# A state-space and gated-GELU layer: half-precision rows turned by DMA instead of by TensorE

## The chip, the cores and the metric

The kernel runs on one core of a Trainium2 chip. The metric is the device time of one execution in microseconds (us), given as the median of several runs. Engines are TensorE (PE), VectorE (DVE), ScalarE (ACT), GpSimd (POOL) and SyncE (SP); SP here only issues DMA transfers.

## The reference, cut to what matters

A sequence x of 2048 rows with 448 channels passes two stages, each behind an adaptive layer norm (scale and shift from a condition vector):

```
h = layernorm(x) * (1 + ca) + sa
x = x + ga * S4(h)                        # long convolution over the sequence, by FFT
h = layernorm(x) * (1 + cb) + sb
g = h @ w_gate ; u = h @ w_up             # 448 -> 1792
x = x + gb * ((gelu(g) * u) @ w_down)     # 1792 -> 448
```

The change lies in the second stage, between the second layer norm and the products with `w_gate` and `w_up`.

## The kernel before

**Stages.** Up to about 385 us the kernel makes the convolution's spectra and the convolution itself. Then the second stage goes through the 2048 rows in four blocks of 512 (`blk` 0 to 3; the change's "blocks two to four" are `blk` 1 to 3). Each block has four row groups of 128 rows (`j` 0 to 3).

**What happens to one row group** (`conv_out`, L1378 to L1494): the last step of the inverse transform on PE and the residual add (L1405 to L1419); the norm on VectorE into a float32 tile `xn` (L1450, task `co.nx`); then the split into two half-precision numbers in one tile `hl` of 128 x 1024. `split_hi` (L1455, task `co.h2`) writes the rounded value into columns 0 to 511, on ScalarE or VectorE as the order says; `split_lo` (L1460, task `co.l2`) writes what is left over into columns 512 to 1023, always on VectorE (a subtraction of 448 columns and a copy of 64). The products need the rows with channels on partitions. So `tr16` (L1466, task `co.t2`) turns the eight 128 x 128 pieces of `hl` on PE into a PSUM tile `pt`, and `out_` (L1473, task `co.c2`) copies that tile into slot `j` of `ht`, a tile of 128 x 8 x 4 x 128 (copies at L481 are ScalarE's, at L483 VectorE's).

**What uses it.** `gate_up` (L1496) makes 14 products per block (`f` 0 to 13; blk 0 does its first four in two halves). A product has 20 matmuls of 128 x 128 by 512 columns (L1528) and four smaller ones (L1522) into the PSUM pair `pq`. ScalarE takes the GELU (L1535), VectorE multiplies (L1542) into `fq`, and `fq` is split once more into `hh` (ScalarE, L1554) and `hlo` (VectorE, L1557) for the product with `w_down` (`down_first` for blk 0, L1597; `down` for the others, L1628 and L1688).

**Buffers.** `hl` has two buffers, `xn` three, `pt` two, `ht` one: a new tile waits until the last reader of the one before it in the ring is done. All but `pt` lie in one pool (`w0`), which is laid over memory that earlier stages have given back.

**Order.** Nothing is scheduled at run time. Every task has a place in the table `PLACE`, and `Plan.order` (L296) sorts all tasks by it; each engine runs its own tasks in that order and waits at each for what it needs. A letter behind a place chooses the engine (a, d, p, s). So blk 1's preparation is woven into blk 0's products: on PE, the last products of blk 0 have places 1549, 1560, 1570 and 1578, the transposes of blk 1 have 1568 (j = 0), 1577 (j = 2), 1590 (j = 3) and 1593 (j = 1), and the first product of blk 1 has 1596. In blk 2 and 3 the row groups are prepared while PE does `down` of the block before.

**SP's queue.** SP issues most transfers, in the order of places too, and stands still at one that must wait. Around blk 1's transposes these are the loads of down weights (`d.ld`, L1735: 1538, 1555, 1569, 1585), a load of gate weights (L1333: 1542), a reload of split weights (`wr.ld`, L1368: 1563, into the three-deep ring `wr`), their store (L1360: 1586) and the next block's convolution result (L1279: 1598).

Of the kernel before, what the change touches and what calls it, by code (L numbers as in the profile page):

```python
# [12 lines left out]
HF = mybir.dt.float16  # L13
# [399 lines left out]
def s4_geglu(ctx: ExitStack, tc: tile.TileContext, a: dict, out: bass.AP):  # L413
    nc = tc.nc
    dma = nc.sync.dma_start
# [31 lines left out]
    POOLS = {"gz": gzs.enter_context(tc.tile_pool(name="gz", bufs=1, side="right")),  # L447
             "ua": uas.enter_context(tc.tile_pool(name="ua", bufs=2, side="right", reuse_waits="tile"))}
# [24 lines left out]
    def add(n, eng, v, fn, deps=(), alloc=(), use=(), table=None, kb=0.0, soft=()):  # L473
        t = plan.add(n, eng, v, fn, list(deps) + list(soft) + [EV.get(GATE.get(b.tag)) for b in alloc], alloc, use, table, kb)
        t.soft = set(soft)
        return t
    EXP, TRIG, ATAN, SQRT, LN = ("exp",), ("trig",), ("atan", "trig"), ("sqrt",), ("ln",)

    def cp(e, dst, src):
        if e == "ACT":  # L480
            A.activation(dst, src, AF.Copy)  # L481
        else:
            V.tensor_copy(dst, src)  # L483

    def sp(n, v, dst, src, kb, deps=(), alloc=(), use=(), q="SP"):
        qf = adma if q == "ACT" else dma
        return add(n, {q: 0.42 if q == "SP" else 0.1}, v, lambda: qf(dst(), src()), deps, alloc, use, kb=kb)
# [890 lines left out]
    def conv_out(blk, t_x, t_y):  # L1378
        xb, yb, hb = X1[blk], YI[blk], Buf("ht")
# [53 lines left out]
        for js in sets:  # L1433
# [9 lines left out]
            t3 = add("co.rc" + z, {"DVE": 0.15}, v0 + js[-1] + 0.3, inv, [t2])  # L1443
            for j in js:
                rst[j] = t3
        cps = []
        for j in range(4):
            xn, pt, hl = Buf("xn"), Buf("pt" if blk else "pd"), Buf("hl")

            def norm(j=j, xn=xn):  # L1450
                xn.tile = POOLS["w0"].tile([128, D], FT, name="xn", bufs=3)
                V.scalar_tensor_tensor(xn.tile, xb.tile[:, j], MV[blk][1][:, j, 0:1], cb1, op0=OP.subtract, op1=OP.mult)
                V.scalar_tensor_tensor(xn.tile, xn.tile, RS[blk][:, j:j + 1], sb, op0=OP.mult, op1=OP.add)

            def split_hi(e, xn=xn, hl=hl):  # L1455
                hl.tile = POOLS["w0"].tile([128, 1024], HF, name="hl")
                cp(e, hl.tile[:, :D], xn.tile)
                cp(e, hl.tile[:, D:512], xn.tile[:, 384:])

            def split_lo(xn=xn, hl=hl):  # L1460
                V.tensor_sub(hl.tile[:, 512:512 + D], xn.tile, hl.tile[:, :D])
                V.tensor_copy(hl.tile[:, 512 + D:], hl.tile[:, 896:512 + D])

            pts = [pt, pt if blk else Buf("pd")]

            def tr16(k0=None, pts=pts, hl=hl):  # L1466
                b = pts[1 if k0 else 0]
                n, k0 = (8, 0) if k0 is None else (4, k0)
                b.tile = POOLS["pd" if n == 4 else "pt"].tile([128, n, 128], HF, name="pd" if n == 4 else "pt")
                for k in range(n):  # L1470
                    T.transpose(b.tile[:, k], hl.tile[:, 128 * (k0 + k):128 * (k0 + k) + 128], K2["ih"])

            def out_(e, k0=None, j=j, pts=pts):  # L1473
                if j == 0 and not k0:
                    hb.tile = POOLS["w0"].tile([128, 8, 4, 128], HF, name="ht", bufs=1)
                ks = slice(0, 8) if k0 is None else slice(k0, k0 + 4)
                cp(e, hb.tile[:, ks, j], pts[1 if k0 else 0].tile)
            vj = v0 + (j + 0.5 if blk == 0 else j + 4.5)
            t1 = add("co.n" + z, {"DVE": 1.38}, vj, norm, [rst[j]], [xn], [xb])
            if blk:  # L1480
                t2 = add("co.h2", {"ACT": 0.8, "DVE": 0.5}, vj + 0.1, split_hi, [t1], [hl], [xn])
                t3 = add("co.l2", {"DVE": 0.7}, vj + 0.2, split_lo, [t2], (), [xn, hl])
                t4 = add("co.t2", {"PE": 0.55}, vj + 0.3, tr16, [t3, c_ih], [pt], [hl])
                cps.append(add("co.c2", {"ACT": 1.05, "DVE": 0.75}, vj + 0.4, out_, [t4] + cps[:1], [hb] if j == 0 else [],
                               [pt] + ([hb] if j else [])))
                continue
            t2 = add("co.h0", {"ACT": 0.7, "DVE": 0.47}, vj + 0.1, split_hi, [t1], [hl], [xn])
            t3 = add("co.l0", {"DVE": 0.8}, vj + 0.2, split_lo, [t2], (), [xn, hl])
            t4 = add("co.ta", {"PE": 0.3}, vj + 0.2, lambda tr16=tr16: tr16(0), [t2, c_ih], [pt], [hl])
            t5 = add("co.ca", {"ACT": 0.5, "DVE": 0.42}, vj + 0.3, lambda e, out_=out_: out_(e, 0), [t4] + cps[:1], [hb] if j == 0 else [],  # L1490
                     [pt] + ([hb] if j else []))
            t6 = add("co.tb", {"PE": 0.3}, vj + 0.3, lambda tr16=tr16: tr16(4), [t3, t4], [pts[1]], [hl])
            cps += [t5, add("co.cb", {"ACT": 0.5, "DVE": 0.42}, vj + 0.4, lambda e, out_=out_: out_(e, 4), [t6, t5], (), [pts[1], hb])]
        CO[blk] = cps  # L1494

# [114 lines left out]
    def down(blk):  # L1610
# [91 lines left out]
        def put(m):  # L1702
# [10 lines left out]
    c_ih = sp("c.ih", 58, lambda: K2["ih"], lambda: a["k_ih"], 32, [EV["end"]])  # L1713
    t_x = x1_load(0, [EV["end"]])
    t_w = add("warm", {"ACT": 0.25}, 58, lambda: A.activation(dump, eps, AF.Sqrt), [EV["end"]], table=SQRT)
    conv_out(0, t_x, YL)
    spin(6, [EV["pq"], c_ih], Buf("pq"), None, lambda: POOLS["ps"].tile([128, 512], FT, name="pq0"),
         lambda t: (K2["ih"], K2["ih"][:, None].to_broadcast([128, 4, 128]), t.rearrange("p (a b) -> p a b", b=128)))
# [39 lines left out]
    for blk in range(4):  # L1758
        for half in range(2 if blk == 0 else 0):
            for f in range(HALF):  # L1760
                gate_up(blk, f, half)
        if blk == 0:
            down_weights(False)
        f0 = 0 if blk else HALF
        for f in range(f0, 14):
            if f % 2 == 0:
                w_load(blk, f // 2) if blk else f // 2 < PRE or weights(f // 2)
            gate_up(blk, f)
            if f == 0 and blk == 1:
                down_weights(True)  # L1770
            if f == f0 and blk < 3:
                conv_out(blk + 1, x1_load(blk + 1, [CO[blk][-1]]), [yi_load(blk + 1)])
        if blk:
            down(blk)
            continue
        for j in range(4):
            down_first(j)
# [54 lines left out]
```

## Time and profile before

| | |
|---|---|
| runs | 796.06, 799.72 and 801.69 us, median 799.72 |
| profiled execution | span 793.8 us from the first to the last instruction; its page gives no further time of its own |
| busy | PE 731.5 us (92%), DVE 594.2 (75%), ACT 466.6 (59%), POOL 9.0 (1%) |
| granted clock of TensorE | 0.995 of full speed over the span |
| DMA | 136.74 MB, mean 172 GB/s |
| the 96 transposes into `pt` (L1471) | 7.0 us of PE busy, between 453.5 and 692.8 us |
| the 12 copies out of `pt` | 7 on ACT of 1.02 us, 5 on DVE of 0.69 us (medians) |

How to read it: a row of a timeline has start, duration, engine, line, operation, what is written from what is read, the shape and how many; in brackets stands how long the engine was idle before it and what ended that. "PEld" is the loading of weights into TensorE, which overlaps with matmuls. The chain of work that ended last has rows of start, duration and what ran; "issue" there is time in which the engine waited for nothing that the profile shows. "SPq" is SP's DMA queue: its rows are the issuing, not the transfer. PE's matmuls overlap, so the chain, which counts each only once, is the view to read PE's time from.

### The profile page before, as it was taken

To read this page: it belongs to the slowest core of one execution; us is meant where nothing else is said; L and a number is where in the kernel's file an instruction comes from. 1 tells how busy PE (TensorE), PEld (TensorE's weight loads), DVE (VectorE), ACT (ScalarE), POOL (GpSimd) and SP (SyncE) were. 2 spreads that over 40 slices of the span, in tenths; PEclk is the share of its full clock that TensorE was granted. 3 is DMA by queue.
4 is the path that set the end of the run, shared out by engine and by line. 5 is a ranking of instruction groups with operands and counts; after the bars stand their busy time and mean duration, and the time that the engine had idled before them with its cause. 6 is when DMAs were issued, how large, how long until landed. Compare 5 with 4: busy or idle time off the path is not lost.

```text
span 793.8 us, 19204 instructions
## 1 busy us (share of the span) xinstructions
PE 731.5 (92%) x8262; PEld 449.3 (57%) x8262; DVE 594.2 (75%) x896; ACT 466.6 (59%) x620; POOL 9.0 (1%) x24
## 2 busy tenths in 40 slices
PE   1866889998999999989999999999999999999998
PEld 0333444443677767678774445444695446944478
DVE  4989999999999999978868851569773587133743
ACT  5699998899999999952645530233412334212330
POOL 0000000000000000002100000000000000000000
PEclk9999999999999999999999999999999999999999
DMA  9554559998888757988797563355307222012201
GB/s 270 172 150 143 152 148 243 284 277 235 232 252 228 219 176 240 299 308 214 234 275 246 205 173 112 127 174 172 131 13 220 93 93 93 2 47 92 82 1 59
DMA packets 91119, 136.74 MB, mean 172 GB/s; under 512 B 21716, under 2 KB 72596, under 8 KB 91034
## 3 DMA queue, kind: packets, MB, share of 16 engines
q1 hardware_dynamic: 85156, 127.32, 53.5%
q10 hardware_dynamic: 5318, 7.22, 2.9%
q8 instruction: 65, 1.06, 0.6%
q0 software_dynamic: 560, 0.98, 0.5%
q14 instruction: 20, 0.16, 0.1%
HBM read 100.39 MB, written 36.01 MB: 172 GB/s over the span
## 4 chain that ended last, share of the span: by engine, by line
PE 64%; DVE 6%; ACT 5%; DMA 3%; issue 3%; SPq 0%; DVEq 0%; ACTq 0%
PE pq L1528 28%; PE pq L1628 9%; PE pd L1597 4%; PE pf L1106 3%; PE kg L749 3%; PE pf L1095 2%; PE kg L772 2%; PE pg L676 2%; PE pq L1522 2%; DMA yi<-y 2%; DVE ty L726 2%; PE pd L1628 2%; PE pd L1405 1%; DVE tx L722 1%; DVE q L1099 1%
## 5 line engine op out<-in xcount | busy, mean ns | idle before, releaser
L1528 PE MATMUL pq<-ht,wr 128*128 128x512 f16 (+1 forms) x1200 | 248.6, 365 | 0.9 <-ACT ge L1535 0.9
L1528 PEld LDWEIGHTS <-wr 128*128 128x128 f16 x1200 | 114.5, 98 | 128.6 <-issue 12.0
L726 DVE TENSOR_TENSOR ty<-my,fg 128x2048 f32<-128x2048 f32 x56 | 127.5, 2283 | 0.9 <-ACT fg L700 0.3
L1542 DVE TENSOR_TENSOR fq<-ge,pq 128x512 f32<-128x512 f32 (+1 forms) x60 | 38.9, 649 | 72.7 <-PE pq L1528 45.6
L1535 ACT ACTIVATE ge<-pq 128x512 f32<-128x512 f32 (+1 forms) x60 | 34.0, 566 | 87.9 <-PE pq L1522 52.8
L1554 ACT ACTIVATE hh<-fq 128x1024 f16<-128x1024 f32 (+1 forms) x49 | 46.7, 961 | 62.2 <-DVE fq L1542 43.6
L1628 PE MATMUL pq<-d,hh 128*128 128x224 f16 x476 | 69.2, 259 | 0.0
L722 DVE TENSOR_TENSOR tx<-mx,fg 128x1024 f32<-128x1024 f32 x56 | 67.7, 1217 | 1.6 <-ACT fg L693 1.0
L749 PE MATMUL kg<-ty,tx 128*32 128x64 f32 x3584 | 62.7, 222 | 4.2 <-DVE tx L722 1.7
L749 PEld LDWEIGHTS kg<-ty,tx 128*32 128x32 f32 x3584 | 53.5, 111 | 22.4 <-issue 12.9
L1557 DVE TENSOR_TENSOR hlo<-fq,hh 128x1024 f16<-128x1024 f32 (+1 forms) x49 | 53.7, 1105 | 15.4 <-ACT hh L1554 15.2
L1628 PE MATMUL pq<-d,hlo 128*128 128x224 f16 x238 | 61.6, 259 | 0.0
L689 ACT ACTIVATE fg<-pg 128x1024 f32<-128x1024 f32 x56 | 58.2, 1039 | 0.8 <-PE pg L676 0.4
L663 ACT ACTIVATE my<-pg 128x1024 f32<-128x1024 f32 x56 | 55.7, 1032 | 2.1 <-PE pg L658 1.9
L1628 PEld LDWEIGHTS <-hh 128*128 128x128 f16 x560 | 54.0, 98 | 0.6 <-issue 0.2
L1106 PE MATMUL pf<-q,fc 128*128 128x160 f32 x264 | 41.5, 307 | 1.2 <-DVE q L1099 1.2
L693 ACT ACTIVATE fg<-fg,small 128x1024 f32<-128x1024 f32 x36 | 41.6, 1172 | 0.1
L1106 PEld LDWEIGHTS pf<-q,fc 128*128 128x128 f32 x264 | 36.4, 190 | 6.6 <-issue 1.5
L676 PEld LDWEIGHTS <-lt 64*128 64x128 bf16 x304 | 17.8, 94 | 37.6 <-issue 25.4
L1745 ACT ACTIVATE d<-fq 128x896 f16<-128x896 f32 x14 | 13.2, 945 | 43.1 <-PE pd L1597 27.3
L676 PE MATMUL pg<-ea,lt 64*128 64x512 bf16 x152 | 30.7, 387 | 7.2 <-ACT fg L700 3.2
L985 PE MATMUL pf<-ui,fu 128*128 128x448 f32 x66 | 31.1, 575 | 1.7 <-ACT uo L481 1.4
(212 smaller groups left out, 1141.3 us busy)
## 6 DMA issues: line engine op xcount, KB each, us to landing
wr<-w_d SPq DMA_DIRECT2D x21, 896.0 KB
fc<-in_k_fc SPq DMA_DIRECT2D x20, 576.0 KB
u_d<-so SPq DMA_DIRECT2D x32, 224.0 KB
ui<-u_d SPq DMA_DIRECT2D x10, 672.0 KB
fq<-in_wd SPq DMA_DIRECT2D x14, 448.0 KB
w<-in_wgu SPq DMA_DIRECT2D x11, 512.0 KB
us<-uo SPq DMA_DIRECT2D x22, 240.0 KB
q<-us SPq DMA_DIRECT2D x22, 240.0 KB
```

The lines of the kernel that those rows point to most:

```text
L663: A.activation(yb.tile.rearrange("p h (n k) -> p n h k", n=2), pb.tile.rearrange("p (n h k) -> p n h k", n=2, h=2), AF.Exp)
L676: T.matmul(pa[:, nh * 512:nh * 512 + 512], w, x, start=(k == 0), stop=(k == 2))
L689: A.activation(fb.tile[:, 0].rearrange("p x (n k) -> p n x k", n=2), pb.tile.rearrange("p (n x k) -> p n x k", n=2, x=2), AF.Sin, scale=TW ...
L693: A.activation(fb.tile[:, 1], fb.tile[:, 1], AF.Sin, scale=-TWO_PI, bias=halfpi)
L722: V.tensor_mul(tx.tile, xb.tile[:, xm, None, :].to_broadcast([128, 2, 512]), fb.tile[:, :, 0])
L726: V.tensor_mul(ty.tile, yb.tile[:, :, None, :].to_broadcast([128, 2, 2, 512]), fb.tile[:, None, :, 1].to_broadcast([128, 2, 2, 512]))
L749: T.matmul(kg[32 * g:32 * g + 32, 2 * (s % 2) + q, :64], tx[:, r, nh, 4 * q + g], ty[:, 0:4:3, nh, 4 * q + g] if r else ty[:, 1:3, nh, 4 * ...
L1106: T.matmul(pz.tile[:, e % 32 - sl0], fc.tile[:, i, 1 + t], pp.tile[:, t, i], start=(t == 0 and e != 32), stop=(t == 1 and e != 0))
L1528: T.matmul(pb.tile[k][:, ts], wr.tile[:, 4 * lo + t, k, c0:c0 + 128], ht[:, m, ts], start=f % 2 == 0 and i == 0, stop=f % 2 == 1 and i == 9)
L1554: A.activation(hg.tile[0][:, cb, c], fq.tile[:, c], AF.Copy)
L1557: V.tensor_sub(hg.tile[1][:, cb, c], fq.tile[:, c], hg.tile[0][:, cb, c])
L1628: T.matmul(bank(k)[:, m], x[:, p, q[0], ts], w[:, p, q[1]], start=new and m == 0 and p == 0 and z == 0, skip_group_check=True, stop=i in ( ...
```

## The change

For blk 1 to 3, the transposes on PE (`co.t2`) and the copies out of PSUM (`co.c2`) go away. In their place one DMA per row group, issued by SP, moves `hl` (128 x 1024, half precision, 256 KB) into slot `j` of `ht` and transposes its eight 128 x 128 pieces on the way. Each has the place of the `split_lo` before it (only blk 3's j = 2 has 1857 instead of 1851, behind j = 0). `hl` gets three buffers and `ht` two. Blk 0 keeps its transposes on PE.

```diff
-    "co.c2": "1588d 1594d 1589d 1592a 1760d 1762d 1774a 1773a 1892a 1906a 1901a 1900a",
...
-    "co.t2": "1568 1593 1577 1590 1756 1758 1769 1771 1877 1904 1868 1895",
+    "co.xt": "1541 1584 1573 1576 1753 1754 1763 1766 1857 1893 1857 1884",
...
             def split_hi(e, xn=xn, hl=hl):
-                hl.tile = POOLS["w0"].tile([128, 1024], HF, name="hl")
+                hl.tile = POOLS["w0"].tile([128, 1024], HF, name="hl", bufs=3)
...
+            def turned(j=j, hl=hl):
+                if j == 0:
+                    hb.tile = POOLS["w0"].tile([128, 8, 4, 128], HF, name="ht", bufs=2)
+                dma(hb.tile[:, :, j], hl.tile, transpose=True)
+
             def out_(e, k0=None, j=j, pts=pts):
                 if j == 0 and not k0:
-                    hb.tile = POOLS["w0"].tile([128, 8, 4, 128], HF, name="ht", bufs=1)
+                    hb.tile = POOLS["w0"].tile([128, 8, 4, 128], HF, name="ht", bufs=2)
...
                 t3 = add("co.l2", {"DVE": 0.7}, vj + 0.2, split_lo, [t2], (), [xn, hl])
-                t4 = add("co.t2", {"PE": 0.55}, vj + 0.3, tr16, [t3, c_ih], [pt], [hl])
-                cps.append(add("co.c2", {"ACT": 1.05, "DVE": 0.75}, vj + 0.4, out_, [t4] + cps[:1], [hb] if j == 0 else [],
-                               [pt] + ([hb] if j else [])))
+                cps.append(add("co.xt", {"SP": 2.0}, vj + 0.4, turned, [t3] + cps[:1], [hb] if j == 0 else [], [hl] + ([hb] if j else []), kb=256))
                 continue
```

## The prediction, made before the changed kernel was run

> **What bounds the kernel now.** I read the page first (spans and busy shares), then the chain of work that ended last from 385 us on, then the timelines of each engine around the transposes, the waits of the DMA queue and the DMA view of single stretches.
>
> ```profile
> span 793.8 us, 19204 instructions
> PE   1866889998999999989999999999999999999998
> ```
>
> TensorE (PE) is busy in nine tenths or more of nearly every slice. The edits touch only blocks two to four (code: blk 1 to 3), which come after 430 us, so their worth is read from the chain there (start, duration, what ran).
>
> ```profile
> 453.66 0.45 PE pt L1471 x8
> ...
> 458.74 0.57 PE pt L1471 x8
> ...
> 464.82 0.62 PE pt L1471 x8
> ...
> 465.47 1.02 ACT ht L481
> ...
> 467.00 4.48 PE pq L1528 x20
> ...
> 584.25 0.89 PE pt L1471 x16
> ...
> 593.19 0.89 PE pt L1471 x16
> 594.08 4.03 PE pq L1628 x42
> 598.11 4.32 PE pq L1528 x20
> ...
> 662.21 0.55 PE pt L1471 x8
> ...
> 692.55 0.45 PE pt L1471 x8
> ...
> 697.02 4.32 PE pq L1528 x20
> ```
>
> Two things are to be seen. The chain is PE nearly without a break, so whatever PE no longer does shortens the run one for one. And the L1471 groups are the transposes that go away: blk 1's four groups lie between 453 and 466 us, blk 2's (two at a time) at 584 and 593, blk 3's from 662 to 693 (four, of which the first and the last are shown; the two between are of 0.45 us like the last). The first gate-up product that needs the transposed rows starts at 467.00, 598.11 and 697.02.
>
> Only ahead of 467.00 does PE also stand still:
>
> ```profile
> 459.38 0.72 ACT L481 ACTIVATE hl<-xn 128x448 f16<-128x448 f32 x2 [4.03 <-PE pt L1471]
> 459.55 4.49 PE L1528 MATMUL pq<-ht,wr 128*128 128x512 f16 x20
> 461.08 1.22 DVE L1557 TENSOR_TENSOR hlo<-fq,hh 128x1024 f16<-128x1024 f32 x1 [2.83 <-ACT hh L1554]
> 462.23 0.62 DVE L1461 TENSOR_TENSOR hl<-xn,hl 128x448 f16<-128x448 f32 x1
> 462.88 0.18 DVE L1462 COPY hl<-hl 128x64 f16<-128x64 f16 x1
> 466.16 0.69 DVE L483 COPY ht<-pt 128x1024 f16<-128x1024 f16 x1 [0.20 <-PE pt L1471]
> ```
>
> The split of the last row group (j = 1) on ScalarE waits 4.03 us for a half-precision buffer ("hl", two of them) that PE's transposes release. Its second half on VectorE ends at 463.06. PE's last product of blk 0 ends at 464.04, then come transposes and copies, and only after the copy that ends at 466.85 does PE go on at 467.00. From 464.04 to 467.00 is 2.96 us, in which 16 transposes lie.
>
> **The change part by part.**
>
> *Removed from PE.* Blk 1: 0.45 + 0.57 + 2.96 = 3.98 us. Blk 2: 0.89 + 0.89 = 1.78. Blk 3: 0.55 + 3 x 0.45 = 1.90. Together 7.66 us, 0.96% of the span: the most that the change can give, since nothing else on the chain is touched.
>
> *Removed from VectorE and ScalarE.* Twelve copies of 0.69 or 1.02 us. They lie beside PE's work, apart from those of blk 1, which the 2.96 us already hold. I count the rest at nothing: PE covers them, and without that cover they would be worth the copies themselves, some 10 us, on engines that here wait for PE.
>
> *The third "hl" buffer, blk 1.* Rows to rebuild the time of the last split:
>
> ```profile
> 451.66 0.95 ACT L1745 ACTIVATE d<-fq 128x896 f16<-128x896 f32 x1 [1.95 <-DMA fq<-in_wd]
> 452.65 1.09 DVE L1748 SCALAR_TENSOR_TENSOR d<-fq,d 128x896 f16<-128x896 f32 x1 [1.02 <-ACT d L1745]
> 454.14 0.72 ACT L481 ACTIVATE hl<-xn 128x448 f16<-128x448 f32 x2 [1.53 <-PE pt L1471]
> ...
> 456.21 0.69 DVE L1453 SCALAR_TENSOR_TENSOR xn<-xn,rs,rows 128x448 f32<-128x448 f32 x1
> 456.82 0.68 DVE L1542 TENSOR_TENSOR fq<-ge,pq 128x512 f32<-128x512 f32 x1
> ...
> 460.01 1.04 ACT L1554 ACTIVATE hh<-fq 128x1024 f16<-128x1024 f32 x1
> ```
>
> The split of j = 2 need no longer wait till 454.14: ScalarE is free at 452.6 and done at 453.3. VectorE is free at 453.74 and makes j = 2's second half by 454.55 (0.80 us), j = 1's normalised row by 455.95 (1.4), the gate product by 456.6 (0.68), j = 3's second half by 457.4. ScalarE splits j = 1 at 456.0 and makes "hh" by 457.8 (1.04); VectorE makes "hlo" by 459.1 (1.22) and j = 1's second half by 459.9, where it was 463.06. So the last transfer of blk 1 can be issued at 459.9. PE, without 1.02 us of transposes, is ready for it at 464.04 - 1.02 = 463.0. The second "ht" buffer is what lets the transfers land while PE still reads blk 0's rows; with one, all four would have to wait till 463.0.
>
> *Memory.* The pool of these tiles grows by 8 KB ("ht") and 2 KB ("hl") per partition, so its tiles and those of the pools opened later lie over other tiles of the earlier stages, whose last readers they wait for. No row shows such a wait ahead of blk 1. I count it at nothing; one on the chain would cost its own length.
>
> *Added: twelve DMA transposes of 256 KB on SP's queue.* No transpose by DMA is in the trace, so its time x from issue to landing is bounded by plain transfers.
>
> ```profile
> 438.25 0.56 SPq L1735 DMA_DIRECT2D fq<-in_wd  x1
> 442.18 0.95 ACT L1745 ACTIVATE d<-fq 128x896 f16<-128x896 f32 x1 [0.80 <-DMA fq<-in_wd]
> 791.02 0.34 ACTq L1710 DMA_DIRECT2D out<-x  x1
> q1 hardware_dynamic: 85156, 127.32, 53.5%
> ```
>
> A load of 448 KB issued at 438.25 released a waiting ScalarE at 442.18: 3.9 us. The last store, 112 KB issued at 791.02, has landed before the span ends: under 2.8 us. On a straight line 256 KB take 3.3 us; 2.8 is the low end. The high end: the rows move in pieces of 128 halves, 256 bytes, so 1024 pieces, and the mean packet of queue 1 took 0.535 x 16 x 793.8 / 85156 = 0.080 us on one of 16 engines. That makes 5.1 us of transfer in place of about 1.3, and x = 7.1. I take x = 4.0, by the row that it is nearest to, the 448 KB load.
>
> [...]
>
> *Where they queue.*
>
> ```profile
> 439.55 0.34 SPq L1333 DMA_DIRECT2D w<-in_wgu  x1
> 440.21 0.18 DVE L1462 COPY hl<-hl 128x64 f16<-128x64 f16 x1
> 447.45 1.04 ACT L1346 ACTIVATE wr<-w 128x1024 f16<-128x1024 f32 x1
> 453.76 9.12 SPq L1735 DMA_DIRECT2D fq<-in_wd  x2
> ```
>
> SP issues in a fixed order and stands still at each transposing transfer until VectorE's second half is there. Blk 1's j = 0 waits till 440.4, and the weight load behind it, issued at 439.55 now, goes about 1.4 us later; ScalarE converts it only at 447.45. j = 2 goes at 454.6, right behind the load at 453.76; j = 3 at 457.4, j = 1 at 459.9. The load behind that one, the second of the row with 9.12 us, waits for the buffer that "hlo" frees (462.3 now, 459.1 then), and loses nothing.
>
> In blk 2 only stores of finished rows and the next convolution's load stand behind the transfers. In blk 3 the loads of the weight ring do:
>
> ```profile
> 654.63 0.63 DVE L1461 TENSOR_TENSOR hl<-xn,hl 128x448 f16<-128x448 f32 x1
> 657.60 0.32 SPq L1368 DMA_DIRECT2D wr<-w_d  x1
> ```
>
> Its j = 0 is ready at 655.5, 2.1 us ahead of the load at 657.60, which itself waits for PE: room for two issues of up to 1 us. I count this at nothing; an issue of 2 us would put that load off by 2 us, and PE still has two loaded weight blocks in the ring of three to work on.
>
> Blk 1 then: j = 1 lands at 459.9 + 4.0 = 463.9, 0.9 after PE is ready. The product that started at 467.00 starts at 463.9: **3.1 us** won.
>
> *Blk 2.* A third buffer is not enough for four row groups: the fourth split waits for the first transfer to land.
>
> ```profile
> 583.38 0.62 DVE L1461 TENSOR_TENSOR hl<-xn,hl 128x448 f16<-128x448 f32 x1
> 588.11 0.50 DVE L483 CAST hl<-xn 128x448 f16<-128x448 f32 x2
> 589.29 0.61 DVE L1638 TENSOR_TENSOR xn<-xn,pq 128x448 f32<-128x448 f32 x1
> ```
>
> With its 0.18 us copy, the second half at 583.38 ends at 584.2, and its transfer lands at 584.3 + x = 588.3. The fourth split, now at 588.11, starts then, its second half is done at 589.6, and its transfer lands at 585.6 + 2x = 593.6. PE, 1.78 us earlier, wants it at 596.3. Behind the waiting split on VectorE stands the residual at 589.29, whose bank PE fills again at 594.08 - 1.78 = 592.3; it slips 0.3 us, of 2.4 to spare. So **1.8 us** won while x stays under 5.4, two lost for each us beyond.
>
> *Blk 3.*
>
> ```profile
> 674.65 0.62 DVE L1461 TENSOR_TENSOR hl<-xn,hl 128x448 f16<-128x448 f32 x1
> ```
>
> The last second half is done at 675.5, PE wants it at 697.0 - 1.9 = 695.1: 19 us of cover, **1.9 us** won.
>
> Sum at x = 4.0: 3.1 + 1.8 + 1.9 = 6.8, so a span of 787.0 us. The page gives no other time for the profiled execution than its span; the runs shown (796.06, 799.72, 801.69) lie 2.3 to 7.9 above it, the median 5.9. So **792.9 us**. At x = 2.8 all 7.7 us are won (792.0). The gain is nought at x = 7.2.
>
> **The rivals.**
>
> *The transfers stand in line* (slower). If one occupies the queue for 5.1 us, as in the high end, and the next follows only then: blk 1's go at 454.6 and land at 461.7, 466.8 and 471.9, 4.9 us after 467.00. Blk 2's first two land at 590.6 and 595.7; the fourth split waits till then on VectorE, and the last two land at 600.8 and 605.9, 7.8 us late. Blk 3 wins 1.9. Net 10.8 lost: **810.5 us**. It decides from some 3.6 us each: with the same 2.0 us around it, blk 1 is then 0.3 late and blk 2 1.6, which eat the 1.9. For it speaks the small piece size; against it that 448 KB are here in 3.9 us.
>
> *Eight blocks one behind the other* (slower). If a transfer is eight blocks of 128 x 128 that each wait for the last, a block costs between one issue (0.56 us) and one short landing (2.8), so 4.5 to 22.4 us; the middle by ratio is 10. Blk 1's would land at 464.6, 474.6 and 484.6 (17.6 late), blk 2's last at 623.5 (25.4 late), blk 3's 0.4 after PE is ready (1.5 won): **841 us**. The trace has no such series to judge by. [...]
>
> *The gap ahead of 467.00 stays* (not slower, little won). If the last split of blk 1 isn't earlier, because the order on ScalarE and VectorE holds it at about 463, its transfer lands at 467 as PE starts today; 3.7 us are won: **796.0 us**. Against it: the 4.03 us wait is for a buffer that is there then.
>
> **How the numbers follow.** Forecast 0.58, gap stays 0.14, in line 0.14, eight blocks 0.14. A measurement of this kernel tells about 1% (8 us) from no change. The greatest gain, 7.7 us, is just inside that, so faster by over 1% gets only 0.08, for scatter; within 1% 0.64; slower by over 1% 0.28, the two slower rivals. The likeliest case's own range is 791 to 797. The range goes down to 790 and up to 812, which takes in the high end of x and leaves out the eight blocks and a little below.
>
> **What would show it.** Right: no L1471 on "pt" in the profile; twelve transposing transfers on SP's queue, 3 to 5 us each; PE's first product of blk 1 some 0.9 us after the last of blk 0, and no gap at all in blk 2 and 3; the 4.03 us wait gone. Wrong: PE waiting for a DMA ahead of the first product of blk 1 by more than 4 us or of blk 2 at all, or SP busy with issuing one transfer for several us, or VectorE waiting for DMA at the fourth split of blk 2 beyond 592.

## The result, and the profile after

The changed kernel takes 789.16 us (median of four runs, 787.92 to 792.09) beside 798.88 us for the kernel before (796.06 to 801.69): ratio 0.989, interval 0.985 to 0.993. A repetition with six runs beside twenty of the kernel before gave 788.73 and 797.99 us, ratio 0.9895, interval 0.9867 to 0.9923. That is a gain of 8.4 us, on the edge of what was called telling (1%, 8 us): the interval holds both sides of it.

The page of the changed kernel, its span and PE's row of the 40 slices:

```profile
span 786.1 us, 19037 instructions
...
PE   1876889998899999989999999999999999999998
```

PE's row is as full as before. The chain of work of the kernel before has one row that the prediction did not show, the product ahead of blk 1's first transposes, and both kernels have an earlier pair of products and a last VectorE operation that serve as marks:

```profile
430.68 8.74 PE pq L1528 x40
...
449.24 4.42 PE pq L1528 x20
```

```profile
790.60 0.39 DVE L1696 TENSOR_TENSOR x<-x,xn 128x224 f32<-128x224 f32 x1
```

The chain of the changed kernel (start, duration, what ran), and its last VectorE operation:

```profile
431.15 8.74 PE pq L1530 x40
...
449.70 8.74 PE pq L1530 x40
458.44 0.54 PE pq L1524 x4
458.98 8.74 PE pq L1530 x40
...
572.44 20.12 PE pq L1630 x210
592.57 4.32 PE pq L1530 x20
...
669.36 20.12 PE pq L1630 x210
689.48 4.32 PE pq L1530 x20
```

```profile
783.06 0.39 DVE L1698 TENSOR_TENSOR x<-x,xn 128x224 f32<-128x224 f32 x1
```

No row on "pt" (L1471) is left in it, and no row of another engine: from 449.70 on PE runs through. A row of 40 matmuls at 458.98 holds the last product of blk 0 and the first of blk 1 without a break; the second half of it starts at 458.98 + 4.42 = 463.40. The stages by these rows:

| from, to | before | after | difference | forecast |
|---|---|---|---|---|
| product ahead of blk 1's preparation to first product of blk 1 (449.24 to 467.00; 449.70 to 463.40) | 17.76 | 13.70 | -4.06 | -3.1 |
| to first product of blk 2 (598.11; 592.57) | 131.11 | 129.17 | -1.94 | -1.8 |
| to first product of blk 3 (697.02; 689.48) | 98.91 | 96.91 | -2.00 | -1.9 |
| to the last VectorE operation (790.60; 783.06) | 93.58 | 93.58 | 0 | 0 |

The sum is 8.00 us, a little more than the 7.66 us that the prediction called the most. The trace is exact enough for this: from the first mark to the last VectorE operation ("the tail" below) the kernel before takes 359.92 us and the changed one 351.91. Ahead of the mark, where the code is the same, executions differ by several us (it lies at 430.68 and 431.15 here, at 436.62 in the repetition), and this is most of the scatter of the times.

Where the 4.03 us wait was, ScalarE and VectorE now show this:

```profile
452.27 0.70 ACT L480 ACTIVATE hl<-xn 128x448 f16<-128x448 f32 x2
...
455.58 0.72 ACT L480 ACTIVATE hl<-xn 128x448 f16<-128x448 f32 x2 [2.13 <-DVE xn L1452]
```

```profile
458.43 0.62 DVE L1460 TENSOR_TENSOR hl<-xn,hl 128x448 f16<-128x448 f32 x1
459.08 0.18 DVE L1461 COPY hl<-hl 128x64 f16<-128x64 f16 x1
```

The split of j = 1 starts at 455.58 as soon as its normalised row is there (VectorE, L1452), no longer when a buffer comes free, and its second half is done at 459.26 where it was 463.06. SP's queue around it, and all twelve transfers in one row (shortest, median and longest issue in ns, first and last in us):

```profile
453.51 0.55 SPq L1737 DMA_DIRECT2D fq<-in_wd  x1
454.30 6.25 SPq L1475 DMA_TRANSPOSE ht<-hl  x3
```

```profile
L1475 SPq DMA_TRANSPOSE ht<-hl x12: 1232/1271/1927, 440.9 to 669.4; - x12
```

The issue of a transposing transfer occupies SP for 1.27 us, that of the plain load ahead of it for 0.55. The three at 454.30 end with that of j = 1 at 460.55, so it was issued at about 459.3 and PE, at 463.40, found it landed. (A transfer is counted here as landed at the last step that the trace shows of its semaphore; for this one that is at 462.36, 3.0 us after the start of its issue. The rows "DMA ht<-hl" further down run from the one to the other.)

In blk 2 the fourth split waits for a transfer, as foreseen, and the residual behind it on VectorE is in time:

```profile
580.29 0.18 DVE L1461 COPY hl<-hl 128x64 f16<-128x64 f16 x1
...
584.43 0.50 DVE L482 CAST hl<-xn 128x448 f16<-128x448 f32 x2 [0.72 <-DMA ht<-hl]
...
585.62 0.61 DVE L1640 TENSOR_TENSOR xn<-xn,pq 128x448 f32<-128x448 f32 x1
```

```profile
579.80 2.65 SPq L1475 DMA_TRANSPOSE ht<-hl  x2
```

The two issues are those of j = 0 and, behind it, j = 1. In the trace the fourth split waits at the semaphore that the first of them raises, and that one is complete at 584.34: **4.6 us** from the start of the issue at 579.80 to its user. (It is not the buffer that was split first, j = 1's, whose transfer landed only at 585.24: what fits this and the run with two "hl" buffers below is that the buffer taken is the one whose transfer has the earliest place in the table.) The DMA view from 579 to 591 us, 0.3 us to a number, shows why this transfer took long:

```profile
GB/s 0 0 0 0 0 0 33 218 214 203 233 139 206 104 9 9 9 156 279 287 260 210 107 0 0 0 107 221 212 204 131 0 0 0 0 0 0 0 0 0
```

From 583.2 to 584.1 hardly anything moves (9 GB/s), with three transfers issued. What held them is open; it is so in the second profile of the changed kernel too (4.9 us to land, 585.26 to 590.15). In blk 1 the transfer of j = 2 took 5.3 us, behind the load of 453.51. The other nine, beside these and the one of 459.3, took 3.0 to 4.1.

### The profile page after: what moved, and what is told of

Same layout as the page of the kernel before. It is cut to its first block, busy times and chain, and to the rows that moved or that the text cites. A ratio compares the mean times of both kernels' runs of the same rounds, so it can differ in the third digit from the quotient of the medians.

```text
span 786.1 us, 19037 instructions
## 1 busy us (share of the span) xinstructions
PE 728.7 (93%) x8166; PEld 445.2 (57%) x8166; DVE 591.4 (75%) x891; ACT 460.1 (59%) x613; POOL 9.0 (1%) x24
## 3 DMA queue, kind: packets, MB, share of 16 engines
q8 instruction: 64, 1.05, 0.5%
## 4 chain that ended last, share of the span: by engine, by line
PE 67%; ACT 13%; DVE 9%; DMA 7%; issue 3%; SPq 1%; ACTq 0%; DVEq 0%
PE pq L1530 29%; PE pq L1630 9%; PE pd L1599 4%; PE kg L748 3%; PE pf L1105 3%; PE pg L675 3%; ACT my L662 2%; DVE ty L725 2%; PE pf L1094 2%; ACT fg L688 2%; PE pq L1524 2%; PE kg L771 2%; DMA yi<-y 2%; PE pd L1630 2%; PE pf L984 1%
```

## The experiments

The theory: the gain is PE's time for the transposes (some 5.6 to 5.8 us) and the end of the standstill ahead of blk 1 (2 us); it depends on transfers that land some 3 us after their issue, and on buffers that let them start early. Rivals: the buffers alone explain the gain; or the transfers cost something that the trace hides. In this table the tail is measured in the profiled execution of each kernel, between the same two operations as above. "Time" is the difference that the ratio of runs makes on 798 us.

| kernel | tail from, to | tail | to the kernel before | time |
|---|---|---|---|---|
| changed, again | 436.62, 788.52 | 351.90 | -8.02 | -8.4 |
| buffers alone | 430.69, 789.42 | 358.73 | -1.19 | -2.3 |
| PE transposes too | 433.13, 790.83 | 357.70 | -2.22 | -3.8 |
| DMA in blk 1 alone | 434.10, 791.25 | 357.15 | -2.77 | -6.2 |
| two "hl" buffers | 437.11, 792.14 | 355.03 | -4.89 | -3.4 |
| one "ht" buffer | 434.17, 795.72 | 361.55 | +1.63 | -0.6 |
| each transfer twice | 432.89, 806.22 | 373.33 | +13.41 | +11.9 |
| transfers in halves | 429.91, 781.81 | 351.90 | -8.02 | one run |

**The changed kernel again.**

> The changed kernel once more, to size the gain. Theory (the gain is the chain time of PE's transposes and of the pause in blk 1): 7.7 us off the kernel before, ratio about 0.990, the same as between the two profiles' spans. Rival (a part of the gain lies elsewhere, for instance in the memory layout of the earlier stages): the 9.7 us between the first medians hold, ratio 0.988 or below.

Measured 788.73 us, ratio 0.9895 (0.9867 to 0.9923). Its profiled execution had a span of 791.5 us, 5.4 more than the one above, and its mark lies 5.47 us later (436.62 beside 431.15): all of that was lost ahead of the second stage's middle, and the tail repeats to 0.01 us. So the gain of 8.0 in the tail stands, and a time difference of 1 or 2 us between kernels says little by itself.

**The buffers alone**, the transposes left on PE:

```diff
-                hl.tile = POOLS["w0"].tile([128, 1024], HF, name="hl")
+                hl.tile = POOLS["w0"].tile([128, 1024], HF, name="hl", bufs=3)
...
-                    hb.tile = POOLS["w0"].tile([128, 8, 4, 128], HF, name="ht", bufs=1)
+                    hb.tile = POOLS["w0"].tile([128, 8, 4, 128], HF, name="ht", bufs=2)
```

> The kernel before with three hl and two ht buffers, transposes still on PE. Theory: the transposes stay on the chain; only the pause ahead of blk 1's first product shrinks (the copies no longer wait for PE's last reading of blk 0, the last second half is done 3 us earlier): 1.1 us below the kernel before, ratio 0.998 to 0.999. Rival (the buffers, not the DMA, brought the gain): 4 us or more below.

Measured 796.13 us, ratio 0.9971 (0.9957 to 0.9985); 1.19 us in the tail. Its chain ahead of blk 1 shows what stays: transposes, a copy, and only then the product.

```profile
464.05 0.91 PE pt L1471 x16
464.98 0.70 DVE ht L483
...
465.82 4.48 PE pq L1528 x20
```

The rival that the buffers bring the gain falls; they bring a seventh of it in the tail, and 2.3 of the 8.4 us by the times.

**DMA, and PE transposing all the same** into PSUM that nobody reads (extra work, the output unchanged):

```diff
+    "co.t2": "1568 1593 1577 1590 1756 1758 1769 1771 1877 1904 1868 1895",
...
+                add("co.t2", {"PE": 0.55}, vj + 0.3, tr16, [t3, c_ih], [pt], [hl])
```

> The changed kernel, and PE still makes the twelve groups of transposes at their old places into PSUM tiles that nobody copies or reads. Theory (PE's time on the chain): 12 groups of 0.45 to 0.57 us come back, 5.6 us above the changed kernel, the pause in blk 1 stays away; ratio to the kernel before 0.997. Rival (the gain came from the copies that left VectorE and ScalarE, or from the waits between engines): within 1 us of the changed kernel, ratio 0.990.

Measured 794.48 us, 5.75 above the changed kernel; in the tail 5.79 above. The transposes stand on the chain again, with nothing between them and the product:

```profile
466.49 0.89 PE pt L1471 x16
467.38 4.32 PE pq L1532 x20
```

So 5.8 of the 8.0 us are PE's own time, and the other 2.2 are the standstill ahead of blk 1. Of these, 1.2 come with the buffers alone; the last 1.0 comes when PE has no copy to wait for (464.96 to 465.82 with the buffers alone) and its product then takes 4.32 us in place of 4.48.

**DMA in blk 1 alone**, blk 2 and 3 by PE:

```diff
-                cps.append(add("co.xt", {"SP": 2.0}, vj + 0.4, turned, [t3] + cps[:1], [hb] if j == 0 else [], [hl] + ([hb] if j else []), kb=256))
+                if blk == 1:
+                    cps.append(add("co.xt", {"SP": 2.0}, vj + 0.4, turned, [t3] + cps[:1], [hb] if j == 0 else [], [hl] + ([hb] if j else []), kb=256))
+                else:
+                    t4 = add("co.t2", {"PE": 0.55}, vj + 0.3, tr16, [t3, c_ih], [pt], [hl])
+                    cps.append(add("co.c2", {"ACT": 1.05, "DVE": 0.75}, vj + 0.4, out_, [t4] + cps[:1], [hb] if j == 0 else [],
+                                   [pt] + ([hb] if j else [])))
```

> Transposes by DMA in blk 1 only; blk 2 and 3 on PE as before, three hl and two ht buffers everywhere. Theory: the gains add up by block, so 4.0 us of the 7.7 are here: 3.7 us above the changed kernel, ratio to the kernel before 0.995. Rival (blk 1's part is hidden by other waits, such as the loads of down weights): less than 2 us below the kernel before, ratio 0.998 or more.

Measured 792.04 us, ratio 0.9922 (0.9902 to 0.9943), 3.3 above the changed kernel, near the 3.7 expected. In the tail it is 5.24 above, because in the profiled execution PE had to wait in blk 1:

```profile
461.86 4.49 PE L1537 MATMUL pq<-ht,wr 128*128 128x512 f16 x20
467.65 4.48 PE L1537 MATMUL pq<-ht,wr 128*128 128x512 f16 x20 [1.30 <-DMA ht<-hl]
```

```profile
456.56 0.95 ACT L1754 ACTIVATE d<-fq 128x896 f16<-128x896 f32 x1 [3.43 <-DMA fq<-in_wd]
```

A load of down weights came late, and ScalarE stood 3.43 us ahead of the splits. The last transfer went at 464.47 and PE took it up at 467.65: 3.18 us. This shows how thin the cover in blk 1 is. In the changed kernel the transfer issued at about 459.3 is there by 462.4, 1.0 us ahead of PE. Without the 1.30 us the tail would be 4.07 us below the kernel before, which is blk 1's 4.06.

**Two "hl" buffers** in the changed kernel (`bufs=3` taken out):

> The changed kernel with two hl buffers instead of three. Theory (the third buffer takes the split of j = 1 out of the line behind a transfer): in blk 1 the split waits for j = 3's transfer to land, 3.2 us after its issue; its own transfer goes out at about the time that PE is ready and lands 3.9 us after it, and blk 2's residual on VectorE comes 0.7 us too late: 4.6 us above the changed kernel, ratio to the kernel before 0.994 to 0.995. Rival (the transfers are so early that the third buffer is idle): within 1 us of the changed kernel, ratio 0.990.

Measured 794.96 us, ratio 0.9958 (0.9935 to 0.9981); in the tail 3.12 above the changed kernel. The mechanism is as expected: ScalarE's split waits for a transfer, PE for the last one (2.0 us), and in blk 2 PE waits 0.8 us for VectorE's residual.

```profile
464.41 0.72 ACT L480 ACTIVATE hl<-xn 128x448 f16<-128x448 f32 x2 [4.91 <-DMA ht<-hl]
```

```profile
459.56 0.55 SPq L1737 DMA_DIRECT2D fq<-in_wd  x1
```

```profile
460.35 3.95 DMA ht<-hl
...
468.15 3.05 DMA ht<-hl
...
471.34 4.48 PE pq L1530 x20
```

```profile
PE pq L1530 <- DMA ht<-hl: 2.0, 1, 2.0
```

The size was less than expected (4.6 us of waits, 2.8 here): the transfer that it waited for was, by its time and its semaphore, the one issued at 460.35, and not the later one that the expectation named; as in blk 2 of the changed kernel, it is the one with the earliest place. That one took 3.95 us, right behind a load of 448 KB, where the one at 468.15 took 3.05.

**One "ht" buffer**, with four "hl" so that the splits need not wait, and blk 1's transfers moved behind PE's last product of blk 0:

```diff
-    "co.xt": "1541 1584 1573 1576 1753 1754 1763 1766 1857 1893 1857 1884",
+    "co.xt": "1588 1594 1589 1592 1753 1754 1763 1766 1857 1893 1857 1884",
...
-                hl.tile = POOLS["w0"].tile([128, 1024], HF, name="hl", bufs=3)
+                hl.tile = POOLS["w0"].tile([128, 1024], HF, name="hl", bufs=4)
...
-                    hb.tile = POOLS["w0"].tile([128, 8, 4, 128], HF, name="ht", bufs=2)
+                    hb.tile = POOLS["w0"].tile([128, 8, 4, 128], HF, name="ht", bufs=1)
```

> One ht buffer instead of two (and four hl buffers, so that the rows can be held), blk 1's transfers placed behind the last loads that blk 0 needs. Theory: the first of the four goes out only when PE has finished with blk 0's rows, each issue takes 1.27 us of SP, the last one lands 3 x 1.27 + 3.25 = 7.1 us after that, with PE idle: 7.1 us above the changed kernel, which is almost all of the gain; ratio to the kernel before 0.998 to 0.999. Rival (transfers overlap in the queue and only the last part of a transfer counts): 4 us above, ratio 0.995.

Measured 798.08 us, ratio 0.9993 (0.9967 to 1.0019): the whole gain is gone. SP waits 3.6 us for PE's last reading of blk 0's rows, then issues all four, and PE waits 7.52 us (7.1 expected).

```profile
466.45 5.50 SPq L1475 DMA_TRANSPOSE ht<-hl  x4
```

```profile
461.93 4.49 PE L1530 MATMUL pq<-ht,wr 128*128 128x512 f16 x20
473.94 6.43 PE L1530 MATMUL pq<-ht,wr 128*128 128x512 f16 x20 [7.52 <-DMA ht<-hl]
```

Each transfer lands 3.2 to 3.4 us after its own issue, and one is issued every 1.4 us: so they overlap. But the DMA view from 467.7 to 473.3 (packets, MB, share of 16 engines) shows that their pieces fill the DMA engines meanwhile:

```profile
q1 hardware_dynamic: 4224, 1.05, 98.6%
```

That is 1.05 MB in 5.6 us, 187 GB/s, or 1.4 us of moving per transfer. SP's issues and the moving are limits of the same size here, and this run cannot tell which of them stands in line. The rest of the 9.64 us in the tail is the next product, which took 6.43 us in place of 4.49; the last section comes back to it.

**Each transfer twice, one behind the other**: a second one to the same place, which waits for the first to land.

```diff
                 dma(hb.tile[:, :, j], hl.tile, transpose=True)
+                dma(hb.tile[:, :, j], hl.tile, transpose=True)
```

> Every transfer is made twice into the same place, the second behind the landing of the first, so that one takes about 6.5 us in place of 3.25 and holds SP for 4.5. Theory (the rival of transfers in line, with this price): blk 1's first product 6.4 us late, blk 2's 7.2, blk 3's in time: 13.6 us above the changed kernel, slower than before, ratio 1.005 to 1.007. Rival (the queue has room for twice the work): within 2 us of the changed kernel, ratio 0.990 to 0.992.

Measured 811.24 us, ratio 1.0149 (1.0121 to 1.0177), 22 above the changed kernel (13.6 expected). PE waits in blk 1 and in blk 2:

```profile
475.14 7.10 PE L1531 MATMUL pq<-ht,wr 128*128 128x512 f16 x20 [9.51 <-DMA ht<-hl]
...
614.21 5.84 PE L1531 MATMUL pq<-ht,wr 128*128 128x512 f16 x20 [7.13 <-DMA ht<-hl]
```

```profile
607.71 3.13 DMA ht<-hl
610.86 3.10 DMA ht<-hl
```

Blk 2's wait is the one expected (7.2), blk 1's is 3 us longer (6.4 expected): by the chain, the doubled transfer of j = 0 (second issue from 445.86 to 447.47) also held back the loads behind it in SP's queue, of gate and of down weights (447.52 and 448.42), and ScalarE's and VectorE's work on them put off the splits.

This is the prediction's slower rival built into the kernel: were transfers of 3.1 us to stand in line in pairs, the kernel would be slower than before.

**Each transfer in two halves** of four blocks:

```diff
-                dma(hb.tile[:, :, j], hl.tile, transpose=True)
+                dma(hb.tile[:, :4, j], hl.tile[:, :512], transpose=True)
+                dma(hb.tile[:, 4:, j], hl.tile[:, 512:], transpose=True)
```

> Every transfer in two, of four 128 x 128 blocks each. If the issue costs by the block, one half takes SP 0.65 us and a row group 1.3 as now, and the time of the run stays; if it costs by the instruction, 1.27 us each and 2.5 a row group, the last of blk 1 lands 1 to 2 us later and PE waits about 0.5 us or more ahead of blk 1.

One run, 786.87 us; the tail is that of the changed kernel. The issue went by the instruction here, not by its blocks: a half took 1.23 or 1.22 us of SP (medians), a whole 1.27.

```profile
L1475 SPq DMA_TRANSPOSE ht<-hl x12: 1189/1234/1335, 438.1 to 666.7; - x12
L1476 SPq DMA_TRANSPOSE ht<-hl x12: 1194/1218/2487, 439.6 to 668.1; - x12
```

The wait of half a microsecond that was expected of the doubled issues did not come. The second half of j = 1 was issued at 459.17 and PE ran on at 462.2, so a half needs less than 3.0 us (by the semaphores most halves land after 2.5).

## Why the prediction was right, and where its sizes were off

**PE's time comes out one for one.** Right, and shown by letting PE transpose all the same: 5.8 us come back. The ceiling of 7.66 was low by 0.34, because taking a group out also removes the break that it makes. The kernel before, on both sides of blk 3's first group:

```profile
661.89 0.32 PE pq L1522 x2
...
662.76 0.32 PE pq L1522 x2
```

Four small matmuls that the transposes cut in two took 0.32 + 0.32 us; uncut they take 0.54 (458.44 above). That happens in blk 1 and blk 3, 0.10 each. The product after the standstill took 4.48 us (467.00) where one in a stream takes 4.32 (592.57): 0.16 more.

**The term for blk 1 was mis-sized**: 3.1 forecast, 4.06 measured. Two numbers in it were too high. The last second half was put at 459.9 in the times of before; it came at 459.26, which is 458.8 when the 0.46 us by which this execution runs later (449.70 for 449.24) are taken off. And x was taken as 4.0, by the 448 KB load; for this transfer it is 3.0, with 3.18 to its user with DMA in blk 1 alone, and 3.05 and 3.1 in the chains with two "hl" buffers and with doubled transfers. The straight line through plain transfers, 3.3, was the better choice for this transfer (not for one behind a load, 5.3, or one held up, 4.5). Either number put right would have had it land just in time (462.9 for 463.0); with both it lands 1.0 us ahead of PE and not 0.9 behind it.

**The high end of x, 7.1, rested on a wrong reading.** It gave each piece of 256 bytes the time of the mean packet of queue 1, 0.080 us. The four transfers in a row with one "ht" buffer (98.6% above) show the pieces themselves: 1.05 MB in 4224 packets are 249 bytes each, and 0.986 x 16 x 5.6 / 4224 = 0.021 us each, so these small packets were quicker than the mean one, and a transfer moves in 1.4 us and not in 5.1. (The 1.3 us that the prediction set beside the 5.1, and with it the 2.0 us around a transfer, is worked out from no row there. The DMA view of the kernel before has a mean of 202 GB/s from 430 to 470 us, at which 256 KB move in 1.3 us.) By landing time, where nothing else is in the way, a transposing transfer lies near the line through the plain ones (256 KB in 3.0 to 3.2 us, 3.3 on the line). Nor is there a price per block to be added up: eight blocks landed in 3.0 to 3.2 us, under the 4.5 that the prediction gave them at the least, and four in 2.5.

**Blk 2: right, with two errors that nearly cancel.** The fourth split waits for the first transfer to land, as forecast, and starts at 584.43, or 588.0 in the times of before (588.3 forecast; 3.60 is added, by which blk 1's first product lies earlier). But the prediction took the issue 0.9 us too late, from the second of two second halves on VectorE (583.38; the first, of j = 0, starts at 582.64), and x 0.5 us too short (4.0 for 4.5). That the two make up for each other is luck. The residual has moved by nothing that PE sees.

**SP's queue: the issue was put at "up to 1 us", it is 1.27.** At 15 us for twelve it still hides, as the unbroken chain shows. Where it does not hide is seen with one "ht" buffer: 5.50 us of issues ahead of PE, with the moving beside them.

**The rivals.** Eight blocks in turn, and transfers in line, fall: with one "ht" buffer four transfers issued from 466.45 on had all landed by 473.94, 7.5 us, where four of 3.1 in line need 12.4. What does stand in line is 1.4 us per transfer, and the rival decides only from 3.6. That the gap stays falls by the changed kernel's chain.

**From span to time.** The prediction added 5.9 us to the span, from three runs of before. A profiled execution's own time lies only 1.8 above its span (787.92 for 786.1, 793.33 for 791.5), and the median of before over twenty runs is 798.0, not 799.72. The forecast time was 3.7 us too high: 0.9 for the span (787.0 for 786.1) and 4.1 for the offset, less 1.2 by which the median of the changed kernel lies above its profiled execution. That the span came out within 0.9 us is luck in part: the second profile of the same kernel has 791.5. The sum of the stages, 8.0 for 6.8, does not depend on that. Because its ceiling lay at 7.7 us, the prediction gave a gain of over 1% a chance of 0.08 only, and both ratios lie just there.

**Open.** The tail is of one execution and the time is a median, and they differ by 1 to 3 us in most variants (buffers alone gain 2.3 for 1.19, blk 1 alone 6.2 for 2.77 or 4.07, two "hl" buffers 3.4 for 4.89). The difference lies ahead of the mark, where executions scatter by some 7 us (the mark lies at 429.9 to 437.1 in the ten profiles), or in waits that the profiled one had by chance. The times went with TensorE's granted clock: of the 23 executions of before beside the last variants, the longest three (801.5 to 802.5 us) have 0.983 to 0.985, the shortest three (795.0 to 795.9) 0.991 to 0.994; the last section shows pauses behind which it was lower. Whether the larger pool moves something in the earlier stages was not tried. Blk 0 by DMA was not tried either.

## What to carry to other kernels

Where PE bounds a stage, count its transposes at their place on the chain: a DMA transpose that starts early enough cost nothing there (from 449 us on, PE waits for no transfer in the changed kernel), though each of these took five times as long as PE's group of eight, or more (3.0 to 5.3 us beside 0.45 to 0.57). What makes it early enough is buffers: the destination needs its own (with one "ht" PE waited 7.52 us), and the source one for each transfer in flight (with two "hl" it waited 2.0). Price a transfer by landing time from plain ones of like size (3.3 us by their line, 3.0 to 3.2 measured), add SP's issue for each instruction (1.27 us for eight blocks, 1.22 to 1.23 for four), and leave room for what moves ahead of it (3.0 us alone, up to 5.3 behind a load in the changed kernel); then look which later loads stand behind it in that queue.

## What the runs showed of the hardware

TensorE's granted clock was lower behind the long pauses. With one "ht" buffer, three stretches behind the pause of 7.52 us (columns: stretch, its length, busy time of PE, PEld, DVE, ACT, POOL with counts, granted clock, DMA share, GB/s):

```profile
474.00:477.00 3.00, 3.00 (x8) 1.08 (x9) 0.00 (x0) 0.00 (x0) 0.00 (x0) 0.50 1.04 253
477.00:480.50 3.50, 3.50 (x16) 1.32 (x14) 0.00 (x0) 0.00 (x0) 0.00 (x0) 0.87 1.05 221
480.50:484.00 3.50, 3.50 (x20) 1.78 (x19) 0.00 (x0) 0.60 (x1) 0.00 (x0) 1.00 1.11 286
```

The granted clock is 0.50, then 0.87, then 1.00, and the product takes 1.9 us longer; after the pauses of 9.51 and 7.13 us (each transfer twice) it took 7.10 and 5.84 us, and behind the second the granted clock was 0.50 too (614.20 to 616.00). After 1.30 us (DMA in blk 1 alone) and 2.0 us (two "hl" buffers) it took 4.48 as ever. The length of a pause alone did not decide it: with two "hl" buffers a pause of 1.8 us at 338 us was followed by half the clock, and the one of 2.0 us at 469 was not (stretch before, stretch behind, for both):

```profile
337.80:341.21 3.41, 1.62 (x51) 0.80 (x40) 2.61 (x3) 1.54 (x3) 0.00 (x0) 1.00 1.03 296
341.21:344.62 3.41, 3.20 (x71) 2.98 (x70) 2.90 (x3) 3.41 (x5) 0.00 (x0) 0.50 0.91 320
467.50:470.91 3.41, 1.86 (x9) 0.66 (x7) 2.84 (x5) 0.80 (x2) 0.00 (x0) 1.00 0.44 79
470.91:474.33 3.42, 2.99 (x14) 1.39 (x15) 1.23 (x1) 1.06 (x2) 0.00 (x0) 1.00 0.98 298
```

PE was busy for 1.62 us of the first stretch and had 0.50 in the next, and it was busy for 1.86 us of the third and had 1.00 in the fourth. What decides between the two is not shown here. So a wait for a late transfer cost its own length plus, in these runs, up to 2.6 us behind it (7.10 beside 4.49), a price that the prediction's slower rivals left out.
